# Sigmoid attention and a token and channel mixer on one core: a c2 pair in each unit's 64x64 run, c1 undivided, and a listed order of PSUM banks in the opening

## The chip, the core and the metric

The kernel runs on one core of one Trainium2 chip. The metric is the device time of one execution in microseconds (us); lower is better. Most executions of a kernel agree within 0.3%.

TensorE (PE) multiplies 128x128 blocks, or four 64x64 blocks at a time, out of SBUF into PSUM. VectorE (DVE) and ScalarE (ACT) read PSUM and write SBUF. GpSimd (POOL) and SyncE (SP) issue most DMAs here. Each engine works through its own queue in the order in which the program gave it instructions, and waits for others by semaphores.

## The reference

Eight batches; 12 heads of 64 for 448 positions; then a mixer with 256 token channels and 1536 channel channels:

```python
scores = scale * np.matmul(q, k.transpose(0, 1, 3, 2)) - np.log(S)
attn = 1.0 / (1.0 + np.exp(-scores))
x = np.matmul(attn, v)            # then heads side by side: (B, S, 768)
...
xt = x.transpose(0, 2, 1)
h = np.maximum(xt @ w_tok1, 0.0) @ w_tok2
u = x + h.transpose(0, 2, 1)
h2 = np.maximum(u @ w_ch1, 0.0) @ w_ch2
return (u + h2).astype(np.float32)
```

There is no sum over a row of scores, so a score can be used as soon as its sigmoid is made.

## The kernel before

**Units.** Work on a batch `b` is cut into three units `u` of four heads each; unit number c = 3b + u, 24 in all. The position index is split as 64 x 7, so a unit's scores are seven pieces `j`.

**Steps of a unit.** `qk(b, u, j)` (line 166) makes scores of piece j with four 64x64 matmuls into one of two `qk` buffers of two PSUM banks each, and ScalarE makes the sigmoid of it into `att` (line 181). `av` (line 191) multiplies by v, seven pieces into two banks, and VectorE copies them to `xT` (line 210). `xtrans_dma` (line 224), or in the opening `xtrans` on TensorE (line 230), gives `xn`, the transpose. `tok_tail` (line 250) and `tok1` (line 268) are the token product; its relu is done by ScalarE (line 293), in the opening by VectorE. `ytrans` (line 295) is the second token product, and VectorE adds it to `xT`, giving `ut` (line 307). `utrans` (line 312) transposes a batch's `ut` by DMA to `un`.

**Channel mixing of a batch.** `ch1` (line 325) makes one of 12 groups (`cb`) of c1, six matmuls of 128x128 with 448 columns, and VectorE makes the relu into `h2` (line 345). `ch2` (line 393) makes one of 6 groups (`t`, `half`) of c2, 12 matmuls of 384 columns; VectorE adds `un` (line 426) and SP sends the result out. `ch2_last` (line 474) does the last 64 positions in tiles of 128x64.

**Pairs.** The same matmuls can be cut into quarters of 64x64 (`quads`, line 349), so that they can stand between score matmuls without a change of tile. Four quarters are in the array together. `ch1_pair` (line 365) does two groups of c1 in this way, `ch2_pair` (line 441) the two halves of one `t` of c2: eight of the 12 blocks as quarters in two turns, and four as large matmuls in `rest` (line 459).

**Loads.** GpSimd issues the loads of q, k, v and weights (line 108 and lines 556 to 584), with a cast to 16 bits. From b=2 on, q and k are regrouped by VectorE (`relayout`, line 119) and transposed by DMA (`dma_transpose`, line 131); `through_dma` (line 137) gives this as eight pieces: three regroupings of k, its transpose, three of q, its transpose. In the loop they are put between pieces of other work. `gated_loads` (line 712) lets POOL wait for q's transpose of the next batch before it loads the one after.

**PSUM banks.** Four banks, `m0` to `m3`, serve everything but scores. `bank` (line 76) hands them out in turn; `keep_open` makes it pass over the bank of a sum that is not yet closed. A bank's new user waits until its old user has been read out. In the loop, `at_bank[0] = ...` sets where the turn goes on.

**Order.** The order is written out by hand. The opening is units 0 to 8: units 0 to 3 (lines 653 to 710), then a loop (line 728) in which shares of batch 0's and batch 1's channel mixing stand between the scores. It asks for 73 banks through c = 7. From c = 9 on (line 800) each unit is a run of 64x64 matmuls (scores, value product of the unit before, a pair, the tail of the token product of the unit before that), then large matmuls: `rest`, `tok1`, `work`, and `ytrans`. What the pair and the work are depends on u: for u=0 the c2 pair of t=0 of batch b-2 and its `ch2_last`; for u=1 the c2 pair of t=1 and both groups of t=2; for u=2 the c1 pair of batch b-1 and its other ten groups. After unit 23 the rest follows in line: the value product of the last unit, c2 of batch 6, the token products, and the whole channel mixing of batch 7 (lines 853 to 873).

Of the kernel before, what the change touches and what calls it, by code (L numbers as in the profile page):

```python
# [9 lines left out]
FP16 = mybir.dt.float16  # L10
FP32 = mybir.dt.float32
# [9 lines left out]
NJ = 7  # L21
NP = 64
NU = 3


@with_exitstack
def kernel(
# [13 lines left out]
    B, H, S, E = q.shape  # L41
# [3 lines left out]
    NDB = D // 128  # L45
# [25 lines left out]

    uts = [pc.tile([128, NDB, 512], FP16, name=f"ut{n}") for n in range(2)]

    at_bank, open_bank = [0], [None]

    def bank(shape, dtype, name):

        if at_bank[0] == open_bank[0]:
            at_bank[0] = (at_bank[0] + 1) % 4
        tag = f"m{at_bank[0]}"  # L80
        at_bank[0] = (at_bank[0] + 1) % 4
        return pp.tile(shape, dtype, tag=tag, bufs=1, name=name)

    def keep_open(is_open):
        open_bank[0] = (at_bank[0] + 3) % 4 if is_open else None

    raw, rel, tr = {}, {}, {}
    att, xn, h1, un = {}, {}, {}, {}
# [236 lines left out]
    def ch1(b, cb, d0=0, d1=NDB):  # L325
        if cb == 0 and d0 == 0:
            h2[b] = pa.tile([128, NCB, S], FP16, tag="h2", bufs=1, name=f"h2_{b}")
        if d0 == 0:
            acc[b, cb] = bank([128, 512], FP32, f"c1_{b}_{cb}")
            keep_open(b != 0 or cb > 1)  # L330
        ps = acc[b, cb]
        for d in range(d0, d1):
            nc.tensor.matmul(  # L333
                out=ps[:, 0:S],
                lhsT=c1[:, BY_UNIT[d], 128 * cb : 128 * cb + 128],
                rhs=uts[b % 2][:, BY_UNIT[d], 0:S],
                start=(d == 0),
                stop=(d == NDB - 1),
            )
        if d1 == NDB:  # L340
            keep_open(False)
            ch1_out(b, cb, ps)

    def ch1_out(b, cb, ps):
        nc.vector.tensor_scalar(  # L345
            out=h2[b][:, cb, :], in0=ps[:, 0:S], scalar1=0.0, scalar2=None, op0=MAX
        )

    def quads(ps, n, turn, lhsT, rhs, first, last):

        for r in range(2):
            p = r ^ turn
            part = slice(64 * r, 64 * r + 64)
            for m in (0, 64):
                nc.tensor.matmul(  # L357
                    out=ps[p][m : m + 64, 0:n],
                    lhsT=lhsT(p, part, m),
                    rhs=rhs(p, part),  # L360
                    start=(first and turn == 0),
                    stop=(last and turn == 1),
                )

    def ch1_pair(b, cb):

        if cb == 0:
            h2[b] = pa.tile([128, NCB, S], FP16, tag="h2", bufs=1, name=f"h2_{b}")
        ps = [bank([128, 512], FP32, f"c1_{b}_{cb + p}") for p in range(2)]

        def step(turn, d):
            quads(
                ps,
                S,
                turn,
                lambda p, part, m: c1[
                    part, BY_UNIT[d], 128 * (cb + p) + m : 128 * (cb + p) + m + 64
                ],
                lambda p, part: uts[b % 2][part, BY_UNIT[d], 0:S],
                d == 0,  # L380
                d == NDB - 1,
            )
            if turn == 1 and d == NDB - 1:
                for p in range(2):
                    ch1_out(b, cb + p, ps[p])

        turns = [[lambda t=t, d=d: step(t, d) for d in range(NDB)] for t in range(2)]
        return turns[0], turns[1], lambda: None

    outs = {}  # L390
    orow = out.rearrange("b (p j) d -> b j p d", j=NJ)

    def ch2(b, t, half, n0=0, n1=NCB):
        cols = slice(DH * half, DH * half + DH)
        if n0 == 0:
            if half == 0:
                outs[b, t] = pa.tile([128, D], FP32, tag="outs", bufs=4, name=f"o_{b}_{t}")
            acc[b] = bank([128, 512], FP32, f"c2_{b}_{t}_{half}")
            keep_open(True)
        ps = acc[b]  # L400
        for cb in range(n0, n1):
            nc.tensor.matmul(  # L402
                out=ps[:, 0:DH],
                lhsT=h2[b][:, cb, 128 * t : 128 * t + 128],
                rhs=c2[:, cb, cols],
                start=(cb == 0),
                stop=(cb == NCB - 1 and b in un),
            )
        if n1 < NCB:
            return  # L410
        keep_open(False)
        if b not in un:
            for n in range(NU):
                nc.tensor.matmul(
                    out=ps[:, 128 * n : 128 * n + 128],
                    lhsT=uts[b % 2][:, NU * half + n, 128 * t : 128 * t + 128],
                    rhs=ident[:, :],
                    start=False,
                    stop=(n == NU - 1),
                )  # L420
        ch2_out(b, t, half, ps)
# [19 lines left out]
    def ch2_pair(b, t):  # L441


        outs[b, t] = pa.tile([128, D], FP32, tag="outs", bufs=4, name=f"o_{b}_{t}")
        ps = [bank([128, 512], FP32, f"c2_{b}_{t}_{p}") for p in range(2)]
        n_quads = 8

        def step(turn, n):
            quads(
                ps,  # L450
                DH,
                turn,
                lambda p, part, m: h2[b][part, n, 128 * t + m : 128 * t + m + 64],
                lambda p, part: c2[part, n, DH * p : DH * p + DH],
                n == 0,
                False,
            )

        def rest():
            for p in range(2):  # L460
                for n in range(n_quads, NCB):
                    nc.tensor.matmul(  # L462
                        out=ps[p][:, 0:DH],
                        lhsT=h2[b][:, n, 128 * t : 128 * t + 128],
                        rhs=c2[:, n, DH * p : DH * p + DH],
                        start=False,
                        stop=(n == NCB - 1),
                    )
                ch2_out(b, t, p, ps[p])

        turns = [[lambda t=t, n=n: step(t, n) for n in range(n_quads)] for t in range(2)]
        return turns[0], turns[1], rest
# [113 lines left out]
    def pieces_ch1(b, cb0=0):  # L586
        for cb in range(cb0, NCB):
            for d in range(0, NDB, 3):
                yield 3 * S, lambda cb=cb, d=d: ch1(b, cb, d, d + 3)
# [6 lines left out]
    def pieces_last(b):  # L596
        for n in range(0, NCB, 3):
            yield 3 * DH, lambda n=n: ch2_last(b, n, n + 3)
# [125 lines left out]
    ON_PE = 2 * NU + 1  # L724

    ONE_RUN = 3 * NU
    pending, copies = [], []
    for c in range(N_FIRST, ONE_RUN):
        b, u = divmod(c, NU)
# [69 lines left out]

    for c in range(ONE_RUN, N_CYCLES):  # L800
        b, u = divmod(c, NU)
        before, ahead = divmod(c - 1, NU), divmod(c - 2, NU)


        lot = b - 1 if u == 2 else b - 2
        at_bank[0] = 2
        if u == 2:
            turn0, turn1, rest = ch1_pair(lot, 0)
            work = pieces_ch1(lot, 2)
        elif u == 0:  # L810
            turn0, turn1, rest = ch2_pair(lot, 0)
            work = pieces_last(lot)
        else:
            turn0, turn1, rest = ch2_pair(lot, 1)
            work = pieces_ch2(lot, [(2, 0), (2, 1)])
        part = len(turn1) * 2 // 3
        qk(b, u, 0)
        qk(b, u, 1)
        for f in turn0:
            f()  # L820
        qk(b, u, 2)
        if u == 2:
            utrans(b - 1)
        av(*before, 0, 4)
        qk(b, u, 3)
        av(*before, 4, NJ)
        xtrans_dma(*before)
        qk(b, u, 4)
        for f in turn1[:part]:
            f()  # L830
        qk(b, u, 5)
        for f in turn1[part:]:
            f()
        at_bank[0] = 0
        tok_tail(*ahead)
        qk(b, u, 6)
        rest()
        tok1(*ahead, with_scores=True)
        at_bank[0] = 2
        if u == 0 and b + 1 < B:  # L840
            copies = through_dma(b + 1, 0)
        for n, (w, f) in enumerate(work):
            f()
            if copies and n % 2 == 1:
                copies.pop(0)()
        at_bank[0] = 0
        ytrans(*ahead)
        if u == 2 and b + 1 < B:
            gated_loads(b)
# [4 lines left out]
    groups = [(t, half) for t in range(3) for half in range(2)]  # L854
    work = [f for w, f in [*pieces_ch2(lot, groups), *pieces_last(lot)]]
    before, ahead = divmod(c - 1, NU), divmod(c - 2, NU)
    av(*before)
    xtrans_dma(*before)
    for f in work[:12]:
        f()  # L860
    tok1(*ahead)
    for f in work[12:16]:
        f()
    tok1(*before)
    for f in work[16:20]:
        f()
    ytrans(*ahead)
    ytrans(*before)
    utrans(B - 1)
    for f in work[20:]:  # L870
        f()
    for w, f in stage2(B - 1):
        f()
# [30 lines left out]
```

## Time and profile before

| | us |
|---|---|
| median of 3 runs | 366.64 (366.64 to 368.11) |
| profiled execution, its own time | 366.46 |
| its span, first to last instruction | 364.7 |
| ScalarE busy | 171.3 (47%) |
| PE line 333 (c1), 516 matmuls | 100.6 |
| PE line 174 (scores), 672 | 60.3 |
| PE line 402 (c2), 336 | 58.1 |
| PE line 201 (value product), 672 | 41.0 |
| PE line 357 (pairs), 640 | 32.0 |
| PE line 486 (last), 192 | 17.3 |
| VectorE line 345 (relu of c1), 96 | 59.2 |

Matmuls overlap: one of 448 columns is listed with 353 ns while the next starts 189 ns after it. So what a stretch of work takes is read from starts, and a wait shows as a longer distance between two starts. The granted clock of TensorE is 0.999 over the span.

A line of a timeline has the start in us, the time until its last instruction ends, the engine, the line of the kernel, the operation, what it writes and reads, and the number of instructions merged into it; in brackets stands the idle time of the engine ahead of it and what ended that. A line of waits has who waited, for whom, the sum in us, how often, and the longest.

### The profile page before, as it was taken

The page shows a single profiled execution, that of the slowest core. Times are in us where ns is not written, and L with a number is a line of the kernel's source. Part 1 is how long each engine was busy: PE and PEld are TensorE (multiplying, and loading weights), DVE is VectorE, ACT ScalarE, POOL GpSimd, SP SyncE. Part 2 cuts the span into 40 slices and gives each one's busy share as a digit, 9 for nine tenths or more (in the row PEclk, how much of TensorE's full clock was granted, in tenths as well). Part 3 has the DMA queues.
Part 4 walks back from the last instruction along what each step waited for, and adds up shares of the span by engine and source line. Part 5 has one row for each costly group of instructions (what it writes and reads, how often), then busy time and mean ns, then how long its engine had stood idle before and what let it go on. Part 6 is the DMA issues. An engine that isn't in the chain of part 4 may idle for free.

```text
span 364.7 us, 8938 instructions
## 1 busy us (share of the span) xinstructions
PE 354.8 (97%) x3968; PEld 207.2 (57%) x3968; DVE 186.2 (51%) x343; ACT 171.3 (47%) x214; POOL 52.8 (14%) x91
## 2 busy tenths in 40 slices
PE   8889999999999999999999999999999999999995
PEld 5555455556556665665655665566656665555563
DVE  3466547355645456455554565455553445525531
ACT  2996545767246770664516761664607751010000
POOL 8875500120120002200040001300010000000000
PEclk9999999999999999999999999999999999999999
DMA  8999999999999398977989497987983274137014
GB/s 146 163 192 203 204 204 193 141 182 213 181 174 162 80 165 157 191 132 154 182 132 215 70 190 149 176 149 147 174 134 81 59 155 43 31 86 130 23 45 108
DMA packets 103958, 52.09 MB, mean 143 GB/s; under 512 B 76016, under 2 KB 100848, under 8 KB 103920
## 3 DMA queue, kind: packets, MB, share of 16 engines
q1 hardware_dynamic: 78880, 29.70, 43.8%
q0 software_dynamic: 24816, 21.50, 38.2%
q8 instruction: 31, 0.51, 0.5%
q10 hardware_dynamic: 224, 0.33, 0.3%
q14 instruction: 7, 0.06, 0.1%
HBM read 43.45 MB, written 11.01 MB: 149 GB/s over the span
## 4 chain that ended last, share of the span: by engine, by line
PE 89%; DMA 4%; POOL 4%; ACT 1%; DVE 0%; issue 0%; POOLq 0%
PE c L333 27%; PE c L402 15%; PE c L357 11%; PE qk L174 9%; PE xa L201 8%; PE yt L300 5%; PE tk L279 5%; PE c L486 5%; PE c L462 4%; DMA raw_q<-in_q_dram 2%; DMA raw_v<-in_v_dram 2%; POOL raw_q L108 1%; POOL raw_k L108 1%; POOL raw_v L108 1%; ACT att L181 1%
## 5 line engine op out<-in xcount | busy, mean ns | idle before, releaser
L181 ACT ACTIVATE att<-qk,att_bias 128x896 f16<-128x896 f32 x168 | 155.6, 1015 | 119.7 <-PE qk L174 119.0
L333 PE MATMUL c<-ut,c 128*128 128x448 f16 x516 | 100.6, 353 | 0.7 <-DVE h L345 0.7
L345 DVE TENSOR_SCALAR h<-c 128x448 f16<-128x448 f32 x96 | 59.2, 623 | 46.9 <-PE c L333 46.0
L333 PEld LDWEIGHTS <-c 128*128 128x128 f16 x516 | 49.6, 98 | 48.4 <-issue 4.4
L174 PE MATMUL qk<-tr_q,tr_k 64*64 64x448 f16 x672 | 60.3, 357 | 2.1 <-ACT att L181 2.0
L402 PE MATMUL c<-c,h 128*128 128x384 f16 x336 | 58.1, 326 | 0.0
L210 DVE CAST xT<-xa 128x448 f16<-128x448 f32 x48 | 27.7, 619 | 40.2 <-PE xa L201 40.2
L426 DVE TENSOR_TENSOR o<-un,c 128x384 f32<-128x384 f16 x42 | 23.3, 554 | 46.1 <-PE c L402 31.0
L402 PEld LDWEIGHTS <-h 128*128 128x128 f16 x336 | 32.1, 98 | 21.7 <-issue 1.8
L201 PE MATMUL xa<-att,raw_v 64*64 64x448 f16 x672 | 41.0, 350 | 0.0
L174 PEld LDWEIGHTS <-tr_k 64*64 64x64 f16 x672 | 22.8, 105 | 21.4 <-issue 15.6
L357 PE MATMUL c<-c,h 64*64 64x384 f16 x640 | 32.0, 323 | 0.0
L307 DVE TENSOR_TENSOR ut<-xT,yt 128x448 f16<-128x448 f16 x48 | 27.5, 614 | 4.4 <-PE yt L300 4.1
L714 POOL COPY gate<-tr_q 128x2 f16<-128x2 f16 x6 | 1.1, 184 | 194.1 <-DMA tr_q<-rel_q 194.1
L201 PEld LDWEIGHTS <-raw_v 64*64 64x64 f16 x672 | 22.4, 107 | 10.7 <-issue 2.2
L293 ACT ACTIVATE h<-tk 128x256 f16<-128x256 f32 x42 | 14.5, 395 | 29.6 <-PE tk L279 29.6
L357 PEld LDWEIGHTS <-h 64*64 64x64 f16 x640 | 19.9, 107 | 8.2 <-DVE o L511 1.5
L300 PE MATMUL yt<-w,h 128*128 128x448 f16 x96 | 22.2, 353 | 0.3 <-DVE h L345 0.3
L279 PE MATMUL tk<-xn,w 128*128 128x256 f16 (+1 forms) x156 | 21.7, 274 | 0.0
L279 PEld LDWEIGHTS <-w 128*128 128x128 f16 (+1 forms) x156 | 14.2, 98 | 6.4 <-issue 3.1
L486 PE MATMUL c<-c,h 128*64 128x384 f16 x192 | 17.3, 328 | 0.0
L108 POOL DMA_DIRECT2D raw_q<-in_q_dram x26 | 16.7, 658 | 3.4 <-DMA w2s<-in_moe_w_tok_dram 1.2
(55 smaller groups left out, 199.5 us busy)
## 6 DMA issues: line engine op xcount, KB each, us to landing
out_dram<-o SPq DMA_DIRECT2D x48, 192.0 KB, 3.0
c<-in_moe_w_ch_dram POOLq DMA_DIRECT2D x4, 1152.0 KB, 15.2
raw_v<-in_v_dram POOLq DMA_DIRECT2D x12, 336.0 KB, 5.6
raw_k<-in_k_dram POOLq DMA_DIRECT2D x10, 336.0 KB, 8.0
raw_q<-in_q_dram POOLq DMA_DIRECT2D x10, 336.0 KB, 10.3
raw_q<-in_q_dram POOLq DMA_DIRECT2D x14, 112.0 KB, 6.1
out_dram<-o SPq DMA_DIRECT2D x15, 96.0 KB, 2.5
raw_k<-in_k_dram POOLq DMA_DIRECT2D x12, 112.0 KB, 5.8
```

Of the source, the lines that this page charges most:

```text
L108: nc.gpsimd.dma_start(out=dst.rearrange("p u hi j e -> p (u hi) (j e)"), in_=heads.rearrange("h (p j) e -> p h (j e)", j=NJ),)
L174: nc.tensor.matmul(out=ps[64 * g : 64 * g + 64, hi, 0:S], lhsT=tr[b, "k"][64 * hi : 64 * hi + 64, u, j, 64 * g : 64 * g + 64], rhs=tr[b, " ...
L181: nc.scalar.activation(out=att[b, u][:, :, j, :], in_=ps[:, :, 0:S], func=SIGMOID, bias=bias_t[:, :], scale=att_scale,)
L201: nc.tensor.matmul(out=ps[g][64 * hi : 64 * hi + 64, 0:S], lhsT=raw[b, "v"][64 * g : 64 * g + 64, u, hi, j, :], rhs=att[b, u][64 * g : 64 ...
L210: nc.vector.tensor_copy(out=xTs[b % 2][:, u, g, 0:S], in_=ps[g][:, 0:S])
L279: nc.tensor.matmul(out=ps[tcb], lhsT=w1[rows, t, cols], rhs=xn[b][rows, u, :, t, :], start=(t == 0 and not with_scores), stop=(t == (2 if ...
L300: nc.tensor.matmul(out=ps[:, 0:S], lhsT=h1[b][:, tcb, g, u, :], rhs=w2[:, tcb, :, :], start=(tcb == 0), stop=(tcb == 1),)
L333: nc.tensor.matmul(out=ps[:, 0:S], lhsT=c1[:, BY_UNIT[d], 128 * cb : 128 * cb + 128], rhs=uts[b % 2][:, BY_UNIT[d], 0:S], start=(d == 0), ...
L345: nc.vector.tensor_scalar(out=h2[b][:, cb, :], in0=ps[:, 0:S], scalar1=0.0, scalar2=None, op0=MAX)
L357: nc.tensor.matmul(out=ps[p][m : m + 64, 0:n], lhsT=lhsT(p, part, m), rhs=rhs(p, part), start=(first and turn == 0), stop=(last and turn = ...
L402: nc.tensor.matmul(out=ps[:, 0:DH], lhsT=h2[b][:, cb, 128 * t : 128 * t + 128], rhs=c2[:, cb, cols], start=(cb == 0), stop=(cb == NCB - 1 ...
L486: nc.tensor.matmul(out=ps[g], lhsT=h2[b][:, n, 384:448], rhs=c2[:, n, DH * g : DH * g + DH], start=(n == 0), stop=(n == NCB - 1 and not ad ...
```

## The change

Four things are done at once.

1. **Banks of the opening.** `OPENING_BANKS`, 73 digits, names the bank of each request in order. `bank` takes these first, and hands out 0, 1, 2, 3 in turn when they are used up. `keep_open` is gone.
2. **Pairs.** Each unit of the loop has the c2 pair of batch b-2 with t = u. `ch1_pair` is gone; u=2 does `ch2_last` of batch b-2 and then all 12 groups of c1 of batch b-1 as large matmuls. Units u=0 and u=1 have no large work beside `rest`, `tok1` and `ytrans`.
3. **Token product.** `tok1` stands right behind the run, ahead of `rest`.
4. **Regrouping of k and q.** Of the eight pieces, two are done behind the third scores of u=1, two behind `rest` of u=1, two behind the third scores of u=2, and two among c1 of u=2.

Behind the loop, one c2 group is done ahead of the last value product, and what follows is moved by one group.

```diff
+OPENING_BANKS = "0321302130213021213021303021302121302130130210321032103210321021301301201"
...
-    at_bank, open_bank = [0], [None]
+    opening_banks = [int(n) for n in OPENING_BANKS]
+    at_bank = [0]
 
     def bank(shape, dtype, name):
 
-        if at_bank[0] == open_bank[0]:
-            at_bank[0] = (at_bank[0] + 1) % 4
-        tag = f"m{at_bank[0]}"
-        at_bank[0] = (at_bank[0] + 1) % 4
-        return pp.tile(shape, dtype, tag=tag, bufs=1, name=name)
-
-    def keep_open(is_open):
-        open_bank[0] = (at_bank[0] + 3) % 4 if is_open else None
+        if opening_banks:
+            n = opening_banks.pop(0)
+        else:
+            n = at_bank[0]
+            at_bank[0] = (n + 1) % 4
+        return pp.tile(shape, dtype, tag=f"m{n}", bufs=1, name=name)
...
-    def ch1_pair(b, cb):
...
+    LATER = 0
...
-        lot = b - 1 if u == 2 else b - 2
-        at_bank[0] = 2
-        if u == 2:
-            turn0, turn1, rest = ch1_pair(lot, 0)
-            work = pieces_ch1(lot, 2)
-        elif u == 0:
-            turn0, turn1, rest = ch2_pair(lot, 0)
-            work = pieces_last(lot)
-        else:
-            turn0, turn1, rest = ch2_pair(lot, 1)
-            work = pieces_ch2(lot, [(2, 0), (2, 1)])
+        X, Y = 2, 0
+        at_bank[0] = X
+        turn0, turn1, rest = ch2_pair(b - 2, u)
         part = len(turn1) * 2 // 3
         qk(b, u, 0)
         qk(b, u, 1)
         for f in turn0:
             f()
         qk(b, u, 2)
+        if copies:
+            copies.pop(0)()
+            copies.pop(0)()
         if u == 2:
             utrans(b - 1)
+        at_bank[0] = Y
         av(*before, 0, 4)
         qk(b, u, 3)
         av(*before, 4, NJ)
...
-        at_bank[0] = 0
+        at_bank[0] = Y
         tok_tail(*ahead)
         qk(b, u, 6)
+        tok1(*ahead, with_scores=True)
         rest()
-        tok1(*ahead, with_scores=True)
-        at_bank[0] = 2
-        if u == 0 and b + 1 < B:
+        if u == 1 and copies:
+            copies.pop(0)()
+            copies.pop(0)()
+        if u == 0 and LATER < b + 1 < B or u == 1 and b + 1 == LATER:
             copies = through_dma(b + 1, 0)
-        for n, (w, f) in enumerate(work):
-            f()
-            if copies and n % 2 == 1:
-                copies.pop(0)()
-        at_bank[0] = 0
+        if u == 2:
+            at_bank[0] = Y + 1
+            for w, f in pieces_last(b - 2):
+                f()
+            at_bank[0] = Y
+            for n, (w, f) in enumerate(pieces_ch1(b - 1)):
+                f()
+                if copies and n % 2 == 1:
+                    copies.pop(0)()
+        at_bank[0] = Y
         ytrans(*ahead)
...
+    at_bank[0] = X
+    for f in work[:4]:
+        f()
     av(*before)
     xtrans_dma(*before)
-    for f in work[:12]:
+    for f in work[4:12]:
         f()
     tok1(*ahead)
-    for f in work[12:16]:
+    for f in work[12:20]:
         f()
     tok1(*before)
-    for f in work[16:20]:
+    for f in work[20:24]:
         f()
     ytrans(*ahead)
     ytrans(*before)
     utrans(B - 1)
-    for f in work[20:]:
+    for f in work[24:]:
         f()
```

More of the change, by code (lines that the diff above doesn't have):

```diff
@@ L329, in ch1 @@
             acc[b, cb] = bank([128, 512], FP32, f"c1_{b}_{cb}")
-            keep_open(b != 0 or cb > 1)
         ps = acc[b, cb]
@@ L340, in ch1 @@
         if d1 == NDB:
-            keep_open(False)
             ch1_out(b, cb, ps)
@@ L363, in quads @@
                 )
-    def ch1_pair(b, cb):
[L367 to L388, printed above, removed]
     outs = {}
@@ L398, in ch2 @@
             acc[b] = bank([128, 512], FP32, f"c2_{b}_{t}_{half}")
-            keep_open(True)
         ps = acc[b]
@@ L410, in ch2 @@
             return
-        keep_open(False)
         if b not in un:
```

## The prediction

> **What bounds the kernel now.** I read the page first, then the chain of waits in order of time, then the timelines of TensorE, ScalarE and VectorE, and last the list of what TensorE waited for.
>
> From the page, busy time of the engines and the costliest line of ScalarE:
>
> ```profile
> PE 354.8 (97%) x3968; PEld 207.2 (57%) x3968; DVE 186.2 (51%) x343; ACT 171.3 (47%) x214; POOL 52.8 (14%) x91
> ...
> L181 ACT ACTIVATE att<-qk,att_bias 128x896 f16<-128x896 f32 x168 | 155.6, 1015 | 119.7 <-PE qk L174 119.0
> ```
>
> TensorE is the bound over the span. The units c = 9 to 23 run from 106.75 to 313.41 us and repeat every 41.4 us. The starts of their runs (first qk of a unit in the timeline of TensorE) are 189.55, 200.03, 212.62 and 230.95, so a u=0 unit takes 10.48 us, u=1 12.59 and u=2 18.33. A gain must come from places where TensorE starts late, so I looked for start-to-start gaps that are longer than the matmul before them (0.189 us for 448 columns, 0.1625 for 384). Timeline of a u=0 unit:
>
> ```profile
> 189.55 0.57 PE L174 MATMUL qk<-tr_q,tr_k 64*64 64x448 f16 x8
> ...
> 195.03 1.47 PE L462 MATMUL c<-c,h 128*128 128x384 f16 x8
> ...
> 196.34 0.82 PE L279 MATMUL tk<-xn,w 128*128 128x256 f16 x6
> ...
> 197.09 2.14 PE L486 MATMUL c<-c,h 128*64 128x384 f16 x24
> ...
> 199.16 0.93 PE L300 MATMUL yt<-w,h 128*128 128x448 f16 x4
> ```
>
> From starts: run 5.48, eight matmuls of `rest` 1.31, tok1 0.75, last 2.07, ytrans 0.87. Between kinds of tile (64*64, 128*128, 128*64) some 0.1 us is lost each time; their number per b stays the same.
>
> Timeline of ScalarE in the u=2 unit that starts at 171.22:
>
> ```profile
> 171.72 6.39 ACT L181 ACTIVATE att<-qk,att_bias 128x896 f16<-128x896 f32 x7 [4.66 <-PE qk L174]
> 177.96 0.70 ACT L293 ACTIVATE h<-tk 128x256 f16<-128x256 f32 x2
> ```
>
> If S is the start of a run, the sigmoids begin at S+0.50 and follow at 0.896 us ((6.39 - 1.015) / 6). The seventh scores need the buffer of the fifth: 0.50 + 4 x 0.896 + 1.015 = S+5.10, and they start at S+5.15 to S+5.19. So a run lasts 5.46 to 5.48 us by ScalarE, whatever pair fills it. Where tok1 stands right behind the run, as it does in this unit, both relus are done at S+7.44.
>
> Timeline of a u=1 unit:
>
> ```profile
> 201.09 1.15 DVE L307 TENSOR_TENSOR ut<-xT,yt 128x448 f16<-128x448 f16 x2
> ...
> 201.98 1.26 PE L201 MATMUL xa<-att,raw_v 64*64 64x448 f16 x16
> ```
>
> The value product's second bank is that of the second y, and VectorE frees it at 202.24 only: the adds of last (199.28) and a regrouping of k (200.44) stand before it in VectorE's queue. That run takes 5.88 to 5.89 us in place of 5.48; for b=7, which has no regrouping, it takes 5.54.
>
> What TensorE waited for, of the whole span:
>
> ```profile
> PE c L333 <- DVE h L345: 0.7, 1, 0.7
> PE tp_q L154 <- DMA raw_q<-in_q_dram: 0.7, 1, 0.7
> PE tp_q L154 <- DVE xT L210: 0.5, 1, 0.5
> PE yt L300 <- DVE h L345: 0.3, 1, 0.3
> ```
>
> These are waits for a bank, all in the opening. The second is put down to a DMA, but that tile's q had landed at 22.67, and its bank (old user: the value product of unit 2) came free at 31.77, against a start at 31.82; I count it as a bank wait.
>
> **Part 1, the opening's banks.** I laid the 73 numbers beside the order in which the opening asks for banks, and took for each the time at which the old user of the new bank is read out in this trace. Five waits go. Transposes of q at 24.73: gap 0.56 over the usual; at 31.82: 0.76. Behind both stands the transpose of xT, which needs VectorE's copies of the same unit (done 25.21 and 32.30), so about 0.5 of each remains as gain. Value product at 40.50: 0.2. The c1 group at 48.38 (bank 0, read out at 48.33): 1.07 - 0.19 = 0.88. ScalarE has idle time from 25.3 us on (0.41, 0.24, 1.05, 0.98 ahead of its next sigmoids), and loads land 2 us or more ahead of use, so nothing there takes the gain back. No number of the list makes a new wait in the opening (least slack 0.06 us, as before).
>
> The list ends with c=7; c=8 goes on from bank 0. Its list ends `...01`: the two y's of c=7 stand in banks 0 and 1, and the next two tiles, the value product of c=8, ask for 0 and 1 again. Before, they got 2 and 3. Timeline around that place:
>
> ```profile
> 86.95 1.14 DVE L509 COPY o<-c 64x384 f32<-64x384 f32 x2 [1.26 <-PE c L497]
> ...
> 88.11 1.56 PE L201 MATMUL xa<-att,raw_v 64*64 64x448 f16 x28
> 88.13 1.15 DVE L307 TENSOR_TENSOR ut<-xT,yt 128x448 f16<-128x448 f16 x2
> ```
>
> VectorE reads the second y until 89.28, as it first has to copy last's two halves. The second bank's first matmul, at 88.15 now, would start at 89.33: **a new wait of 1.18 us**. Everything of c=8 stands behind it on TensorE. At the end of c=8 the y's then find banks 0 and 1 two c1 groups old, in place of just filled: the gap of 0.69 at 106.28 becomes 0.19, -0.50. Opening: -0.5 - 0.5 - 0.2 - 0.88 + 1.18 - 0.50 = **-1.40 us**. Bounds: +0.7 if the first four come to nothing, -2.6 if the new wait doesn't come.
>
> **Part 2, pairs in the loop.** Per b: the 24 undivided c2 matmuls of u=1 go (3.90 by their row at 166.47 to 170.37); the third c2 pair's run costs 5.48 for 5.46 (+0.02) and its `rest` 1.31; the two c1 groups that were a pair are 12 matmuls at 0.189 (the 60 of u=2 take 11.35): 2.27. Sum -0.30. What goes is the old pair's idle: it had 0.3 us less to do than ScalarE left it time for.
>
> [...] Per b there are 16 more 64*64 matmuls and 4 fewer large ones. In the rows, 32 quarter matmuls of 384 columns take 1.30 us (189.95 to 191.25), that is four in 0.1625, the same as one large one of the 24 in 3.90, so I charge nothing. [...]
>
> **Part 3, last and tok1.** Last moves from u=0 to u=2 with its own 2.07 us and its changes of tile: nothing. With it VectorE's adds leave the place ahead of the u=1 run, and k's regroupings go behind the third scores: the y adds then end about S+1.0, 0.9 ahead of the value product, so the 0.41 us of u=1 goes (0.06 for b=7). In u=2 one regrouping stands before the y adds, which end near S+1.6 against a value product at S+1.9.
>
> Tok1 before `rest`: TensorE is at ytrans (u=0, 1) or at last (u=2, bank 1, which a relu reads) at S + 5.48 + 0.66 + 1.31 = S+7.45; the relus end at S+7.44. Cover and work are equal; I charge 0.03 us for each, 0.10 per b. Before, last and the c2 groups covered this.
>
> Last now stands before c1, in bank 1. Its adds end 1.26 us after it (199.16 to 200.42 in the rows), and the second c1 group asks for bank 1 after 1.135: **+0.17 per b**, a new wait. VectorE's queue behind holds only the c1 read-outs, with four banks in turn.
>
> Queues: POOL's loads wait for q's transposes, which move from 8.7 us after the start of u=2 to about 12, in a u=2 that is 6 us longer; loads land some 2 us earlier against the next u=0. SP: k's transposes (3.66) now stand just before un's (5.08) and the u=2 xn (1.26), which is wanted 20 us later; the u=0 xn landed 5.8 us after its issue and is wanted 8.3 after. Nothing charged; a late xn would stall the token product.
>
> Sum of parts 2 and 3: -0.30 - 0.41 + 0.10 + 0.17 = -0.44 for four b's, -0.09 for the last: **-1.85 us**. Bounds: 0 if the covers fall short by 0.12 us in 15 units, -2.8 without the charged waits.
>
> **Part 4, the end.** A c2 group goes ahead of the value product. TensorE has no wait there now (gaps all under 0.16 us), and later tiles have 0.3 us of slack or more by the same reckoning: 0.
>
> **Sum.** -3.25 on a profiled execution of 366.46 us (span 364.69 and 1.77 around it): 363.2. The median, 366.64, lies 0.18 above that execution; I say 363.3.
>
> **Rivals.**
> - *The opening's four waits come back* behind ScalarE or a load: part 1 is +0.68, the total -1.17, 365.4. For: ScalarE was without a gap to 25.3 us. Against: its idle time after.
> - *The loop gains nothing*: new bank waits eat it, -1.40, 365.2. For: two covers that are equal to 0.01 us.
> - *ScalarE becomes the bound of the short units* (the other side). u=0 and u=1 shrink to about 8.32 us and hold seven sigmoids and two relus, 7.44 by the rows. If the relus come half a sigmoid later (0.45), ytrans (in u=2: last) waits that long in 15 units: +6.75 - 3.25, 370.1. It decides from 0.22 us of delay on. Against: 7.44 was measured in a unit with this very order, and ScalarE is idle again 1.3 us before the next sigmoid.
> - *The wait at c=8 doesn't come*: -4.4, 362.2. Against: the bank numbers.
> - *Small matmuls cost more*: weight loads take 107 ns for 64*64 and 98 for 128*128; if the 9 ns showed in 16 more per b, +0.7, 364.0. [...] No row shows it.
>
> **Chances.** Forecast 0.53, opening lost 0.14, loop lost 0.10, ScalarE 0.12, no wait at c=8 0.07, small matmuls 0.04. The measurement tells 0.5% (1.8 us) from no change: faster, under 364.8, gathers the forecast, the two last and part of the middle ones: 0.70; within 0.5% 0.18; slower 0.12. The range reaches from below the case without the wait to above the two lost ones: 361.8 to 365.8.
>
> **What would show it.** Right: starts of units at about 8.3, 8.3 and 24.2 us; runs of 5.48 in u=1; no gap before c1 at 47 us; a gap of 1.2 us in the value product near 87 us; a gap of 0.17 between the first and second c1 group. Wrong: u=0 and u=1 above 8.8 us with ytrans behind a relu, or a token product that waits for xn.

## The result, and the profile after

| | before | changed |
|---|---|---|
| median of 4 runs each, us | 367.38 (366.64 to 368.40) | 363.65 (362.98 to 364.64) |
| ratio, 95% interval | | 0.991 (0.9884 to 0.9937) |
| profiled execution: time, span | 366.46, 364.7 | 364.3, 362.5 |
| from the start of a unit to the next (u=0, 1, 2) | 10.48, 12.59, 18.33 | 8.30, 8.30, 24.27 |
| loop, from the run of c=9 to the first matmul behind c=23 | 206.66 | 204.24 |
| behind the loop, to the end of the span | 51.28 | 51.34 |

The change makes the kernel 3.7 us faster by the medians, where 3.3 was forecast. In some executions of both kernels, that of the changed kernel's profile among them, the mean granted clock is 0.993 or 0.994 and the time some 1.3 to 1.8 us longer: in that profile TensorE is granted half its clock for 3.41 us in the opening (19.85 to 23.26 us; last section). So the two spans differ by 2.2 us only. At full clock, before takes 366.4 to 367.0 us in the runs below and the changed kernel 363.0: 3.6 us less.

One change of tile, 0.09 us behind the last ytrans, lies in the loop before and behind it in the changed kernel, where a c2 group with the same tile follows. Like for like, the loop is 2.33 us shorter and the rest the same within 0.03.

The page of the changed kernel, engines and the chain by engine:

```profile
PE 354.4 (98%) x4028; PEld 203.4 (56%) x4028; DVE 185.3 (51%) x343; ACT 169.4 (47%) x214; POOL 52.9 (15%) x91
...
PE 94%; ACT 4%; DVE 1%; issue 0%
```

TensorE is still the bound, busy for 354.4 us where it was 354.8, in a shorter span. Timeline of a u=0 unit and of what follows:

```profile
188.68 0.57 PE L175 MATMUL qk<-tr_q,tr_k 64*64 64x448 f16 x8
...
194.16 0.83 PE L280 MATMUL tk<-xn,w 128*128 128x256 f16 x6
194.83 1.46 PE L434 MATMUL c<-c,h 128*128 128x384 f16 x8
195.42 0.70 ACT L294 ACTIVATE h<-tk 128x256 f16<-128x256 f32 x2
...
196.13 0.92 PE L301 MATMUL yt<-w,h 128*128 128x448 f16 x4
196.81 1.15 DVE L308 TENSOR_TENSOR ut<-xT,yt 128x448 f16<-128x448 f16 x2
...
196.98 0.57 PE L175 MATMUL qk<-tr_q,tr_k 64*64 64x448 f16 x8
...
197.87 1.14 DVE L120 COPY rel_k<-raw_k 128x896 f16<-128x896 f16 x2
...
198.87 0.93 PE L202 MATMUL xa<-att,raw_v 64*64 64x448 f16 x16
```

The relus end at 196.12, and ytrans starts at 196.13: work and cover are equal, as the sum had it, and nothing is lost. In the next unit the y adds end at 197.96, the regroupings come behind them, and the value product at 198.87 takes 0.93 where it took 1.26.

The opening of the changed kernel, at the value product of c=8:

```profile
86.48 1.14 DVE L481 COPY o<-c 64x384 f32<-64x384 f32 x2 [1.26 <-PE c L469]
...
87.23 0.57 PE L175 MATMUL qk<-tr_q,tr_k 64*64 64x448 f16 x8
...
87.66 1.15 DVE L308 TENSOR_TENSOR ut<-xT,yt 128x448 f16<-128x448 f16 x2
...
88.33 0.38 PE L202 MATMUL xa<-att,raw_v 64*64 64x448 f16 x2 [0.52 <-DVE ut L308]
88.86 1.51 PE L202 MATMUL xa<-att,raw_v 64*64 64x448 f16 x26 [0.15 <-DVE ut L308]
...
90.49 3.77 PE L333 MATMUL c<-ut,c 128*128 128x448 f16 x19
```

The same stretch in the kernel before, from the unit's first scores to its first c1 group:

```profile
87.70 0.57 PE L174 MATMUL qk<-tr_q,tr_k 64*64 64x448 f16 x8
...
89.79 4.71 PE L333 MATMUL c<-ut,c 128*128 128x448 f16 x24
```

This is the new wait: the first bank comes free at 88.28, the second at 88.81. In the value product two starts are 0.68 and 0.34 us later than usual, and the whole stretch takes 3.26 us (87.23 to 90.49) where it took 2.09: 1.17 more. What TensorE waited for in the whole span:

```profile
PE qk L175 <- ACT att L182: 2.0, 5, 0.5
...
PE xa L202 <- DVE ut L308: 0.7, 2, 0.5
```

The waits for q's transposes, for c1 and for ytrans are gone from this list, and the value product's is new.

### The profile page after: what moved, and what is told of

The parts are those of the page before. It is cut to its first block, busy times and chain, and to the rows that moved or that the text cites. A ratio compares the mean times of both kernels' runs of the same rounds, so it can differ in the third digit from the quotient of the medians.

```text
span 362.5 us, 9065 instructions
## 1 busy us (share of the span) xinstructions
PE 354.4 (98%) x4028; PEld 203.4 (56%) x4028; DVE 185.3 (51%) x343; ACT 169.4 (47%) x214; POOL 52.9 (15%) x91
## 4 chain that ended last, share of the span: by engine, by line
PE 94%; ACT 4%; DVE 1%; issue 0%
PE c L333 30%; PE c L356 11%; PE c L375 10%; PE qk L175 9%; PE xa L202 8%; PE tk L280 6%; PE c L434 5%; PE yt L301 5%; PE c L458 5%; ACT att L182 4%; PE heat L582 2%; PE tp_k L155 1%; PE tk L261 1%; PE tp_q L155 1%; DVE ut L308 0%; PE xb L235 0%
## 5 line engine op out<-in xcount | busy, mean ns | idle before, releaser
L333 PE MATMUL c<-ut,c 128*128 128x448 f16 x576 | 112.7, 353 | 0.0
L333 PEld LDWEIGHTS <-c 128*128 128x128 f16 x576 | 54.7, 98 | 55.7 <-issue 4.9
L175 PE MATMUL qk<-tr_q,tr_k 64*64 64x448 f16 x672 | 57.2, 358 | 2.1 <-ACT att L182 2.0
L356 PE MATMUL c<-c,h 64*64 64x384 f16 x960 | 46.6, 323 | 0.0
L202 PE MATMUL xa<-att,raw_v 64*64 64x448 f16 x672 | 39.9, 353 | 0.7 <-DVE ut L308 0.7
L375 PE MATMUL c<-c,h 128*128 128x384 f16 x216 | 37.8, 326 | 0.0
L356 PEld LDWEIGHTS <-h 64*64 64x64 f16 x960 | 28.1, 107 | 11.8
L175 PEld LDWEIGHTS <-tr_k 64*64 64x64 f16 x672 | 20.3, 105 | 22.2 <-issue 15.6
L375 PEld LDWEIGHTS <-h 128*128 128x128 f16 x216 | 20.4, 98 | 14.5 <-issue 1.8
L202 PEld LDWEIGHTS <-raw_v 64*64 64x64 f16 x672 | 20.4, 108 | 12.2 <-issue 1.9
L434 PE MATMUL c<-c,h 128*128 128x384 f16 x120 | 22.0, 326 | 0.0
```

The costliest lines, as they stand in the source:

```text
L175: nc.tensor.matmul(out=ps[64 * g : 64 * g + 64, hi, 0:S], lhsT=tr[b, "k"][64 * hi : 64 * hi + 64, u, j, 64 * g : 64 * g + 64], rhs=tr[b, " ...
L202: nc.tensor.matmul(out=ps[g][64 * hi : 64 * hi + 64, 0:S], lhsT=raw[b, "v"][64 * g : 64 * g + 64, u, hi, j, :], rhs=att[b, u][64 * g : 64 ...
L333: nc.tensor.matmul(out=ps[:, 0:S], lhsT=c1[:, BY_UNIT[d], 128 * cb : 128 * cb + 128], rhs=uts[b % 2][:, BY_UNIT[d], 0:S], start=(d == 0), ...
L356: nc.tensor.matmul(out=ps[p][m : m + 64, 0:n], lhsT=lhsT(p, part, m), rhs=rhs(p, part), start=(first and turn == 0), stop=(last and turn = ...
L375: nc.tensor.matmul(out=ps[:, 0:DH], lhsT=h2[b][:, cb, 128 * t : 128 * t + 128], rhs=c2[:, cb, cols], start=(cb == 0), stop=(cb == NCB - 1 ...
L434: nc.tensor.matmul(out=ps[p][:, 0:DH], lhsT=h2[b][:, n, 128 * t : 128 * t + 128], rhs=c2[:, n, DH * p : DH * p + DH], start=False, stop=(n ...
```

## The experiments

The parts were taken apart first: the list alone, everything but the list, the regrouping alone.

**The list alone, on the kernel before.**

```diff
...
-    at_bank, open_bank = [0], [None]
+    opening_banks = [int(n) for n in OPENING_BANKS]
+    at_bank, open_bank = [2], [None]
...
     def bank(shape, dtype, name):
...
+        if opening_banks:
+            return pp.tile(shape, dtype, tag=f"m{opening_banks.pop(0)}", bufs=1, name=name)
...
-        open_bank[0] = (at_bank[0] + 3) % 4 if is_open else None
+        open_bank[0] = (at_bank[0] + 3) % 4 if is_open and not opening_banks else None
```

Behind the list the turn starts at bank 2, so that c=8 gets the banks that it had before.

> The kernel before with the 73 listed banks in its opening and nothing else; from c=8 on banks go on as before. Theory (the list's gain is the four bank waits that it removes): the waits at 24.7, 31.8, 40.5 and 48.4 us go, -0.5 -0.5 -0.2 -0.9 = -2.1 us, no wait in the value product of c=8, and the first run of the loop starts 2.1 us earlier than 106.75. Rival (the opening is held by ScalarE until 25 us and gives part back): -1.1 us. Rival (the opening's stall goes to a load): 0.

Measured 364.77 us (364.41 to 366.04), ratio 0.9927 (0.9902 to 0.9952). At full clock it takes 364.7 and before, in the same comparison, 366.6: -1.9 for -2.1 expected. In its profile, which has the half clock, the loop starts at 106.31 us, so the 2.1 can't be read off its starts. Its waits of TensorE:

```profile
PE qk L178 <- ACT att L185: 2.0, 5, 0.5
...
PE yt L304 <- DVE h L349: 0.3, 1, 0.3
```

Of the bank waits only that of ytrans at the end of c=8 is left, which the expectation left in. The rivals at -1.1 and 0 are out: neither ScalarE nor a load took the gain back.

**Everything but the list.** The opening hands out banks in turn again, with `keep_open`.

> The changed kernel with its opening as before, banks in turn, so that only the loop and the end are changed. Theory: the loop gains alone, units of 8.3, 8.3 and 24.3 us, -2.3 us against before (before's loop took 206.66 us, the changed one 204.33); the opening ends at 106.75 as before. Rival (the loop's gain needs the opening's): less than 1 us.

Measured 364.42 us (364.21 to 364.44), ratio 0.9919 (0.9896 to 0.9941): -2.2. Units take 8.30, 8.30 and 24.26 us, and the loop starts at 106.88. So the loop's gain needs nothing of the opening's. Its waits also settle whom q's transposes waited for:

```profile
PE tp_q L155 <- DVE xT L211: 1.2, 2, 0.7
```

The opening is that of before, and this profile puts both long waits down to VectorE's copies. In the profile of before, one of the two was put down to a DMA; packets of a later load were just landing in the same moment there. A load that landed 9 us earlier, and a bank read out 0.05 us earlier, were the better evidence.

**The regrouping of k and q alone, on the kernel before.**

```diff
         qk(b, u, 2)
+        if copies:
+            copies.pop(0)()
+            copies.pop(0)()
...
+        if u == 1 and copies:
+            copies.pop(0)()
+            copies.pop(0)()
...
-            if copies and n % 2 == 1:
+            if u == 2 and copies and n % 2 == 1:
```

> The kernel before with the regrouping of k and q alone put where the change has it (behind the third scores of u=1 and u=2, behind the large matmuls of the pair in u=1). Theory (of the 0.41 us that u=1 loses, the regrouping ahead of the y adds is 0.35): the run of u=1 takes 5.54 us in place of 5.88 in all b's, -0.34 in four of them, -1.4 us against before. Rival (last's adds alone hold the bank): 5.88 stays, no change.

Measured 365.44 us (365.05 to 367.39, 12 runs), ratio 0.9961 (0.9942 to 0.998): -1.3 at full clock, for -1.4 expected. u=1 takes 12.26 in every b, as only b=7 did before. Timeline of VectorE and TensorE at the start of a u=1 unit:

```profile
198.79 1.14 DVE L511 TENSOR_TENSOR o<-un,c 64x384 f32<-64x384 f16 x2 [2.18 <-PE c L486]
...
199.96 1.15 DVE L307 TENSOR_TENSOR ut<-xT,yt 128x448 f16<-128x448 f16 x2
...
201.03 1.14 DVE L119 COPY rel_k<-raw_k 128x896 f16<-128x896 f16 x2
...
201.50 0.93 PE L201 MATMUL xa<-att,raw_v 64*64 64x448 f16 x16
```

The y adds end 0.39 us before the value product starts; where the regrouping stood ahead of them, they ended 0.26 after. Four times 0.33 is 1.3 us, over half of the 2.33 that the loop gains: what this place in VectorE's queue is worth.

**The token product behind `rest` again, on the changed kernel.**

```diff
-        tok1(*ahead, with_scores=True)
         rest()
+        tok1(*ahead, with_scores=True)
```

> The changed kernel with the token product behind the pair's large matmuls again (order of before), all else as changed. Theory (the order is what covers the relus): tok1 ends 1.3 us later, the relus end at 8.03 us after the start of the run as in before's u=0 in place of 7.44, ytrans waits some 0.4 us in u=0 and u=1 and last's bank 0.5 us in u=2: units of 8.7, 8.7 and 24.8, +6.5 us against the changed kernel, slower than before. Rival (the earlier read-out of the pair makes up for it, VectorE sets the pace): within 1 us of the changed kernel.

Measured 370.03 us (369.98 to 370.11), ratio 1.0084 (1.0058 to 1.0111). Units of 8.76, 8.76 and 24.80: +7.0 against the changed kernel, slower than before. In a u=0 unit:

```profile
196.85 0.82 PE L280 MATMUL tk<-xn,w 128*128 128x256 f16 x6
197.38 0.71 ACT L294 ACTIVATE h<-tk 128x256 f16<-128x256 f32 x2 [0.43 <-PE tk L280]
197.82 1.07 PE L301 MATMUL yt<-w,h 128*128 128x448 f16 x4
```

ytrans stands behind the relus, so that each short unit takes 0.46 us longer; in u=2, 0.53 longer, last waits for them (2.4 us in five waits of TensorE). This is the rival on the other side made real. It shows that moving the large work out of u=0 and u=1 is only worth something with the token product ahead of `rest`.

**Last in u=0 again, on the changed kernel.** `pieces_last(b - 2)` runs in u=0, in bank 2; u=2 has c1 alone behind its pair.

> The changed kernel with last done in u=0 again (behind the pair's large matmuls, in bank 2), u=2 having c1 alone behind its pair. Theory (moving last is worth next to nothing by itself; the regrouping's place and the pair are what the loop gained): u=0 10.45, u=1 8.36 (last's adds hold the value product's bank by 0.06, as in before's b=7), u=2 22.0, together -0.1 us per b against the changed kernel, as the 0.16 us gap in c1 goes too. Rival (last in u=0 was what held the bank in u=1): u=1 at 8.7, +0.3 per b.

Measured 362.49 us (362.43 to 364.34), ratio 0.9888 (0.9848 to 0.9927), at full clock 0.5 below the changed kernel's 363.0. Units 10.54, 8.36, 21.92, sum 40.82 for 40.87: about half of the 0.5 (5 x 0.05). So moving last earned nothing; u=1 gives 0.06 back, and the gap in c1 goes.

**Last in bank 2, on the changed kernel.** `at_bank[0] = X` in place of `Y + 1` ahead of last.

> The changed kernel with last of u=2 in bank 2 (the pair's first, read out about when last starts) in place of bank 1. Theory (the 0.16 us gap between the first and second c1 group is last's read-out out of bank 1): the gap goes, u=2 takes 24.1 in place of 24.27, -0.8 us in all. Rival (VectorE's queue sets the gap): 24.27 stays. Rival (the pair's read-out is late): last starts later, 24.3 or more.

Measured 363.36 us (362.50 to 364.16, three of six with the half clock), ratio 0.9902 (0.9878 to 0.9925); at full clock 0.5 below 363.0, for 0.8 expected. u=2 takes 24.16 for 24.27. The gap of 0.16 between the first and second c1 group is gone (all starts there are 0.19 apart). But last starts 1.46 us behind the pair's large matmuls in place of 1.40, as the pair's first bank is read out only at 170.57, when last could have started. So the mechanism of the second rival is true as well, at a smaller size.

**The banks of c=8.**

```diff
+OPENING_BANKS += "3201320132010123"
```

> The changed kernel with 16 more digits in the list, so that the value product of c=8 gets banks 3 and 2, read out long before, and all banks of c=8 are named. Theory (the wait of c=8 is one of banks): the two gaps of 0.68 and 0.34 us at 88.3 and 88.9 go and the time falls by 1.0 us against the changed kernel. Rival (VectorE sets the pace there, and the wait moves to c1 behind it): under 0.3 us.

Measured 361.79 us (361.60 to 363.43), ratio 0.986 (0.9833 to 0.9887). At full clock 361.65, that is 1.35 less than the changed kernel; the two profiles, both with the half clock, are 1.1 apart. The same place in the timeline:

```profile
87.29 0.57 PE L176 MATMUL qk<-tr_q,tr_k 64*64 64x448 f16 x8
...
87.69 1.56 PE L203 MATMUL xa<-att,raw_v 64*64 64x448 f16 x28
87.71 1.15 DVE L309 TENSOR_TENSOR ut<-xT,yt 128x448 f16<-128x448 f16 x2
...
89.37 1.88 PE L334 MATMUL c<-ut,c 128*128 128x448 f16 x9
```

The value product now starts ahead of the y adds and waits for nothing. From the unit's first scores to c1 it takes 2.08 us for 3.26: the whole wait of 1.18 is gone, and VectorE doesn't take it back.

**Both mends together, and both with work for TensorE in the opening.** The second kernel also has nine matmuls on zeros in three waits of TensorE for ScalarE between 16 and 20 us (`keep_warm(3)` behind the scores 2, 3 and 5 of unit 1, in bank 1, by one more digit in the list).

> The changed kernel with the 16 more listed banks for c=8 and last of u=2 in bank 2. Theory: both gains add, -1.3 and -0.8 us against the changed kernel, 360.9. Rival: the second one is nothing, 361.65.

> The kernel with both bank mends, and nine more matmuls on zeros in the opening (three each in three waits of TensorE for ScalarE between 16 and 20 us, into a bank of their own). Theory (the half clock that some executions show for 3.41 us from 19.8 us on comes of TensorE's idle time in the window before): no execution shows it any more, all lie within 0.4 us, near 360.9, and the dear ones, 1.5 us above, are gone. Rival (it comes of something else, or so few matmuls are too few): some executions still show it.

Measured 361.24 us (361.05 to 362.99), ratio 0.9858 (0.9834 to 0.9882), for the first: at full clock 361.1, so the gains add. The second takes 361.09 us (361.04 to 361.31), ratio 0.9842 (0.982 to 0.9864). Its median is the lowest of all kernels here, 5.5 us below before and 2.6 below the changed kernel; at full clock the two are the same.

## Why the prediction was right

- **Part 1, waits that go.** -2.1 forecast for the four ahead of c=8, -1.9 measured with the list alone. Reading the wait at 31.82 us against the profile's own attribution was right: with the same banks, the profile of everything but the list puts it down to VectorE.
- **The wait at c=8.** 1.18 forecast; the timelines show 1.17 with the wait against before, and 1.18 against other banks. It was read off the end of the list alone: two tiles just filled, and a turn that goes back to their banks.
- **The opening in sum.** -1.40 forecast. Three kernels below with the changed opening and a profile at full clock start the loop at 105.33, 105.42 and 105.66 us, three with the old opening at 106.75, 106.88 and 106.94: -1.4 between the means.
- **Part 2, pairs.** A run of 5.48 us whatever pair fills it: all 15 units show 5.48 or 5.49. No run has the pairs alone. But with last back in u=0, u=2 differs from before by its new pair and by c1 undivided alone, and it takes 3.59 us more than before (21.92 for 18.33), where 3.60 was charged; u=1 takes 4.23 less, the 3.90 of its c2 groups and the 0.33 of the regrouping. The 16 more small matmuls per b cost nothing that can be seen: 32 quarters of 384 columns take 1.30 us between starts in both kernels (189.95 to 191.25 before, 189.08 to 190.38 changed), four the time of one large matmul (0.1625). The last rival's 9 ns for each of the 16 (107 for 98 in the rows of weight loads) would be 0.14 us in u=2, where 3.59 stands against 3.60.
- **Part 3.** u=1's 0.41 came from two causes as forecast (0.33 regrouping, 0.06 last). The c1 gap of 0.17 is there with 0.16. The 0.10 per b charged at ytrans and at last did not come: that term was mis-sized, and it is why the loop gained 2.33 in place of 1.85. Here a relu that ended 0.01 us ahead of its user was early enough. q's transposes start 13.3 us into u=2 (164.41 to 177.74), not at about 12 as forecast; nothing waits for that.
- **Part 4.** 51.28 us behind the loop before, 51.25 without the change of tile that moved there: nothing, as forecast.
- **Sum.** -3.25 forecast, -3.6 measured at full clock. The difference is the 0.5 us of part 3; the other terms came out within some 0.2 us, so the sum does not rest on errors that cancel. The half clock was not in it, since the profile of before has none in its opening.

## What to carry to other kernels

Ask for every buffer who used it last and when that one was read out, and hand out the one that has been free longest; a list that ends must be followed past its end, as the next user may ask for the two newest (1.18 us at c=8). In a queue that works in order, put what nobody waits for (a regrouping for the next batch) behind what frees a buffer (1.3 us here). Before work is moved out from between a producer and its user, work out both times from the rows: here they met within 0.01 us, and two steps in the other order cost 7.0 us, about twice the whole gain.

## What the runs showed of the hardware that was not expected

TensorE is granted half its clock for one stretch of 3.41 us in the opening of some executions. Stretches of the changed kernel's profile (us, busy time of PE, PEld, DVE, ACT and POOL with instructions, granted clock, share and rate of DMA):

```profile
16.40:19.85 3.45, 1.95 (x28) 0.93 (x23) 2.11 (x4) 3.45 (x5) 2.00 (x4) 1.00 1.24 191
19.85:23.26 3.41, 3.41 (x28) 1.76 (x28) 1.26 (x3) 2.19 (x3) 3.41 (x6) 0.50 1.18 178
```

In the 3.45 us before, TensorE waits for ScalarE and is busy for 1.95, and then it runs at 0.50. The profile of before has the same 1.95 between 16.40 and 19.85 us and goes on at 1.00. The clock records of the two differ in where their stretches begin. In all eleven traces each stretch at full clock is a whole number of 3.413 us long: 4, 99, 100, 104, 105 or 106 of them (before 358.40 us, that is 105; the changed kernel 13.65 and 337.92, that is 4 and 99). The first one begins 6.11 to 6.19 us into the span in the three profiles with the half clock there (the changed kernel, at 6.19, the list alone, the banks of c=8), and at 3.89 to 5.71 in the other eight (before at 5.58). If each trace is cut into steps of 3.413 us from there, the one ahead of the half clock has TensorE busy for 1.91 to 1.98 us in the three (the changed kernel: 1.91, from 16.43 to 19.84 us), while the opening of the other eight has no step below 2.29 (before: 2.33, from 15.82 to 19.24 us). So the same waits fall into one step or are spread over two. That this decides is the author's reading of the eleven traces: no run here sets where the steps begin, and what sets the clock is not shown.

Busy time alone does not tell the steps apart. The kernel with both mends has one with 1.58 us near its end (353.87 to 357.28) and runs on at full clock. There the tiles are large, in the opening they are mostly quarters. If each matmul counts with the share of the array that it fills (0.189 us for 448 columns of a 128x128 tile, a fourth of it for 64x64), the three steps hold 1.0 to 1.2 us, that one 1.3 and the poorest of before's opening 1.4. This is an estimate from the rows, and no rule is shown by it.

With the nine added matmuls the same stretches read:

```profile
16.40:19.85 3.45, 3.25 (x40) 1.83 (x33) 2.05 (x4) 3.45 (x5) 1.65 (x3) 1.00 1.26 198
19.85:23.26 3.41, 3.41 (x44) 1.73 (x47) 1.85 (x4) 3.36 (x4) 3.41 (x6) 1.00 0.94 130
```

None of four executions of that kernel had the half clock. That the added work prevents it is not shown. Of the kernels without it, 25 of 89 executions had a mean clock of 0.993 to 0.995, which goes with the half clock (6 of 17, 3 of 11 and 2 of 7 of before); at that rate four without it come by chance one time in four. Everything but the list had none in six, and the token product behind `rest` none in four, both without added matmuls. And in the profile with the added matmuls the first stretch at full clock begins at 5.53 us, as it does in that of everything but the list, so steps cut from there spread these waits over two anyway.
